# Quarter units in an expert stage: remainders of up to 32 tokens as four column tiles, and another order of the units

## The chip, the core and the metric

One Trainium2 chip, one of its cores. A core has TensorE (PE; its weight loads are listed apart as PEld), VectorE (DVE), ScalarE (ACT), GpSimd (POOL) and SyncE (SP), which run their own instruction streams and wait for each other by semaphores; sixteen DMA engines move data. The metric is the device time of one execution in microseconds; of the kernel before, three runs took 794.92, 795.33 and 796.32 us (median 795.33).

## The reference, cut to what matters

Attention with pooled queries, a gated feed-forward layer (FFN), and then a mixture of experts over 1152 tokens, the part that the change touches:

```python
def _moe2_ref(x, w_gate, w_noise, noise, w1, w2):     # x 1152 x 512, 8 experts, F = 1024
    noisy_logits = x @ w_gate + np.log1p(np.exp(x @ w_noise)) * noise
    top2 = np.argpartition(-noisy_logits, 2, axis=1)[:, :2]
    ...                                               # softmax over the two: top2_w
    for e in range(E):
        for k in range(2):
            mask = top2[:, k] == e
            h = np.maximum(x[mask] @ w1[e], 0.0)      # 512 -> 1024
            out[mask] += top2_w[mask, k, None] * (h @ w2[e])
```

With the reference's inputs (seed 0) the eight experts get 317, 56, 55, 668, 166, 97, 924 and 21 tokens (counted by running the reference). Which tokens go where is only known on the chip at run time.

## The kernel before, in words

The program is one static instruction list per engine. Attention runs to about 270 us, the FFN to about 530 us, and the expert stage from there to the end. Routing (logits, top two, ranks, tables) is worked out in small steps between the matmuls of the FFN and of the first expert unit.

**Blocks and units.** The tokens of each expert are ranked and cut into blocks of 128. A *unit* is one or two blocks of one expert, with that expert's weights (two matrices of 2 MB, loaded in eight pieces of 512 KB). There are fourteen units, numbered 0 to 13, whose kinds are fixed in the list `SEQ`:

- **P**, a pair of blocks (the second with more than 64 tokens): 256 columns at a time.
- **Q**, a full block and a remainder of up to 64 tokens, the *half*.
- **S**, a single block of more than 64 tokens; **H**, a half alone.

Which expert and which tokens a unit gets is data: `r_blocks` gives every pair of blocks a kind by comparing the expert's count with thresholds (`thrs`), ranks the pairs of each kind (`pos`, by a matmul with a triangle), and selects expert numbers (`eb`, `ti`) and token numbers (`gidx`, `sidx`; for halves `gidxh`, `sidxh`, from `r_index`). `NSTAT` says how many units of each kind the static list has. If some kind has more, `more` is 1 and a branch at the end runs further units. Units 0 and 1 are pairs chosen early, from the first 512 tokens.

**P, Q and S blocks** multiply in three passes of split numbers (high and low part, `fp32r`): each weight piece is rounded by ACT (`w_hi`, L106) and subtracted by DVE (`w_lo`, L1037); eight pieces a unit. This split runs five pieces ahead of PE (`LEAD`). Pieces 0 to 3 are up-projections (L1112 for pairs, L1127 for single blocks), pieces 4 to 7 down-projections (L1139).

**Halves** use the weights as loaded (`RAW`, plain fp32; each such matmul is two instructions in the trace). `up_half` (L1147) puts two groups of 64 tokens' results in two column tiles: partitions 0 to 63 take one weight piece, 64 to 127 another. `hh_trans` transposes the result (PE L1158, then a copy, L1162 or L1164). `down_half` (L1171) puts output columns 0 to 255 of the 64 tokens in one column tile and 256 to 511 in the other.

**Order and queues.** `units()` is written out in program order. Two sets of weight buffers, for even and odd units, are reloaded on SP's queue for unit u+2 as unit u frees them: after the split of a piece (P, S), or after `up_half` and `down_half` (Q, H; `reload`). `finish(u)` scales the result (DVE L1201) and adds it into the output in DRAM by an indirect DMA (a scatter, POOL L1202); it stands in the program within unit u+1. All scatters write the same tensor, so each waits until the one before has landed. `gather_x` (POOL L1058) fetches tokens three units ahead, and `x_trans` transposes them (PE L1002, or L1083 for halves).

```python
SEQ = [("P", None)] * 2 + [("P", 0), ("P", 1), ("H", 0), ("P", 2), ("H", 1), ("P", 3), ("Q", 0), ("H", 2), ("Q", 1),
                           ("H", 3), ("Q", 2), ("S", 0)]
```

Of the kernel before, what the change touches and what calls it, by code (L numbers as in the profile page):

```python
# [21 lines left out]
def fused_kernel(ctx, tc, q, k, v, w_gate, w_val, w_out, rms_g,  # L22
                 r_gate, r_noise, noise, e_w1, e_w2, out, dbg=None):
    nc = tc.nc
    P = 128
# [865 lines left out]
    def r_blocks():  # L891
        v, u = rtile("v01", [P, 4]), rtile("u6", [P, 6], BF16)
        ncol = PB["n"][0:NCOL]
        v0, va, vb, mn = (v[0:NCOL, i:i + 1] for i in range(4))
# [14 lines left out]
        pos = rtile("pos", [P, 6])[0:NCOL]  # L909
        pe.matmul(pq[0:NCOL, 0:6], R["lt"][0:NCOL, 0:NCOL], u[0:NCOL], start=True, stop=True)  # L910
        dve.tensor_copy(pos, pq[0:NCOL, 0:6])
# [2 lines left out]
        dve.tensor_tensor(sel, R["i128"][0:NCOL, None, 0:NA].to_broadcast([NCOL, 6, NA]),
                          pos[:, :, None].to_broadcast([NCOL, 6, NA]), op=ALU.is_equal)
        dve.tensor_tensor(sel, sel, kinds[:, :, None].to_broadcast([NCOL, 6, NA]), op=ALU.mult)
# [647 lines left out]
```

## Time and profile before

| | |
|---|---|
| median of three runs | 795.33 us |
| the profiled execution | 794.49 us |
| its span in the trace | 792.6 us |
| PE busy | 758.6 us, 96% of the span |
| DVE, ACT, POOL busy | 525.9, 377.8, 255.2 us |
| PE's granted clock, mean | 0.987 of full speed |
| weight loads of the experts | 112 of 512 KB |

The span runs from the first to the last instruction; 1.9 us of the execution lie around it. Times in the rows are from the span's start. A busy PE is one that has a matmul in flight; how fast it goes is read from the distance between starts. In a timeline, adjacent instructions of one line are merged: the second number is the length of the whole run and xN the number of instructions. "[0.70 <-ACT hs L1130]" says that the engine sat idle for 0.70 us and what ended it.

### The profile page before, as it was taken

The numbers are of one execution on the slowest core, as the hardware profiler recorded it, in microseconds if no ns is written. First come the engines' busy times: TensorE is split into PE (matmuls) and PEld (weight loads), VectorE is DVE, ScalarE is ACT, GpSimd is POOL, SyncE is SP. The second block draws the span as 40 slices with busy tenths as digits, with TensorE's granted clock in tenths as the row PEclk, the third lists the DMA queues.
The fourth block names the chain that finished last, engine by engine and source line by source line (L and its number), as shares of the span: only waits on it lengthen the run. The fifth ranks groups of instructions, "written<-read, shape, count | busy, mean of one in ns | idle before, by whom it ended". The sixth has DMA issues, their size and how long they took to land. (4 is left out here: it accounts for less than half of the span.)

```text
span 792.6 us, 13276 instructions
## 1 busy us (share of the span) xinstructions
PE 758.6 (96%) x5008; PEld 626.4 (79%) x5008; DVE 525.9 (66%) x791; ACT 377.8 (48%) x770; POOL 255.2 (32%) x221
## 2 busy tenths in 40 slices
PE   5999999999999989999999999999999999999993
PEld 4877777777776679988888789997999787877782
DVE  6678778777779867656577745579766564563562
ACT  3665655656667644443242325265535252453460
POOL 8456266375723421222012400102312322313222
PEclk9899999999999999999999999999999999999997
DMA  7344231322131311333023100773997999569922
GB/s 220 88 134 154 63 105 41 95 76 60 46 122 54 107 54 54 107 106 106 14 97 111 51 31 24 258 250 116 350 333 236 265 315 340 169 209 344 330 51 30
DMA packets 72728, 113.28 MB, mean 143 GB/s; under 512 B 7281, under 2 KB 37551, under 8 KB 72656
## 3 DMA queue, kind: packets, MB, share of 16 engines
q1 hardware_dynamic: 67504, 101.55, 39.6%
q0 software_dynamic: 5152, 10.80, 6.1%
q8 instruction: 41, 0.67, 0.4%
q14 instruction: 31, 0.25, 0.1%
HBM read 98.16 MB, written 9.85 MB: 136 GB/s over the span
## 5 line engine op out<-in xcount | busy, mean ns | idle before, releaser
L536 PE MATMUL gv<-XN,ws 128*128 128x256 f32 (+2 forms) x912 | 165.1, 331 | 0.9 <-POOL ws L402 0.9
L536 PEld LDWEIGHTS gv<-XN,ws 128*128 128x128 f32 x912 | 143.7, 189 | 15.0 <-issue 1.8
L193 DVE TENSOR_REDUCE Ql<-s 128x1 fp32r<-128x1152 f32 x72 | 97.3, 1354 | 55.8 <-PE s L188 33.7
L1037 DVE TENSOR_TENSOR wz<-raw,wz 128x1024 fp32r<-128x1024 f32 x80 | 95.9, 1222 | 46.7 <-ACT wz L106 46.5
L204 ACT ACTIVATE et<-st 128x288 f32<-128x288 f32 x288 | 103.5, 417 | 41.4 <-PE st L203 38.9
L202 PE MATMUL st<-QH,KT 128*128 128x288 f32 x288 | 92.3, 335 | 2.4 <-ACT et L204 1.0
L402 POOL TENSOR_TENSOR ws<-wm,ws 128x1024 fp32r<-128x1024 f32 x18 | 43.9, 2437 | 154.5 <-ACT ws L401 139.6
L1139 PE MATMUL py<-wz,hTT 128*128 128x512 f32 x384 | 93.5, 395 | 0.0
L557 PE MATMUL po<-ws,hT 128*128 128x512 f32 x324 | 83.2, 395 | 2.2 <-DVE X L562 2.1
L203 PE MATMUL st<-QlT,KT 128*128 128x288 f32 x288 | 81.8, 298 | 0.0
L106 ACT CAST wz<-raw 128x1024 fp32r<-128x1024 f32 x80 | 81.3, 1046 | 0.8 <-PE py L1139 0.5
L1139 PEld LDWEIGHTS py<-wz,hTT 128*128 128x128 f32 x384 | 70.2, 188 | 13.9
L229 PE MATMUL av<-et,v 128*64 128x288 f32 x576 | 77.4, 412 | 0.5 <-ACT xT L234 0.5
L202 PEld LDWEIGHTS st<-QH,KT 128*128 128x128 f32 x288 | 54.7, 190 | 22.0 <-issue 12.3
L557 PEld LDWEIGHTS po<-ws,hT 128*128 128x128 f32 x324 | 58.9, 188 | 14.2 <-DVE X L562 3.2
L217 DVE TENSOR_TENSOR es<-es,et 128x576 f32<-128x576 f32 x64 | 62.5, 976 | 1.5
L229 PEld LDWEIGHTS av<-et,v 128*64 128x64 f32 x576 | 38.4, 136 | 27.8 <-issue 3.9
L1202 POOL DMA_INDIRECT out_dram<-yo,sidx x16 | 27.3, 1709 | 98.5 <-DVE yo L1201 52.8
L1112 PEld LDWEIGHTS ph<-xgT,wz 128*128 128x128 f32 x480 | 57.9, 188 | 1.0 <-issue 0.8
L1112 PE MATMUL ph<-xgT,wz 128*128 128x256 f32 x480 | 58.4, 282 | 0.0
L203 PEld LDWEIGHTS st<-QlT,KT 128*128 128x128 f32 x288 | 55.2, 192 | 0.1
L546 ACT CAST hT<-sl 128x256 fp32r<-128x256 f32 (+2 forms) x38 | 18.9, 497 | 74.6 <-DVE sl L545 74.6
(282 smaller groups left out, 1135.3 us busy)
## 6 DMA issues: line engine op xcount, KB each, us to landing
raw<-in_moe_w_dram SPq DMA_DIRECT2D x112, 512.0 KB, 8.6
wraw<-in_moe_w_gate_dram SPq DMA_DIRECT2D x6, 1024.0 KB, 5.2
wraw<-in_moe_w_val_dram SPq DMA_DIRECT2D x6, 1024.0 KB, 5.1
wraw<-in_moe_w_out_dram SPq DMA_DIRECT2D x6, 1024.0 KB, 5.0
kraw<-in_k_dram SPq DMA_DIRECT2D x16, 288.0 KB, 4.0
v<-in_v_dram SPq DMA_DIRECT2D x8, 576.0 KB, 4.1
KT<-KT SPq DMA_DIRECT2D x16, 288.0 KB, 3.2
Qraw<-in_q_dram SPq DMA_DIRECT2D x16, 256.0 KB, 4.0
```

The source lines that it names most:

```text
L106: act.copy(o, i)
L193: dve.tensor_reduce(Ql[p % 3][h][:, c, D:D + 1], t[:, :, 0:384], axis=AX.XY, op=ALU.max, negate=True)
L202: pe.matmul(t[:, 0:NG], KT[p, h][:, cs], QhT[p, h][:, n0:n0 + NG], start=True, stop=False)
L203: pe.matmul(t[:, 0:NG], KT2[h][p % NKT[h]][:, cs], QlT[p, h][:, n0:n0 + NG], start=False, stop=True)
L204: act.activation(et[:, h, :], t[:, 0:NG], AF.Exp, scale=SCALE)
L217: eng.tensor_tensor(acc, acc, e, op=ALU.add)
L229: pe.matmul(av[h * D:(h + 1) * D, 0:NG], V[p][:, h, c, :], ET[p, g, c][:, h, :], start=(c == 0), stop=(c == KC - 1))
L536: pe.matmul(t[:, 0:n], w[a][:, d, j * P:(j + 1) * P], XN[hf][b_][:, d, cs], start=(k_ == 0), stop=(k_ == 11))
L557: pe.matmul(pt, HT[f, hf][a][:, j, c0:c0 + P], w[b_][:, j, :], start=(k_ == 0), stop=(k_ == 5))
L1037: eng.tensor_tensor(lo, RAW[u % 2][i], hi.bitcast(F32), op=ALU.subtract)
L1112: pe.matmul(o, w[a][:, d, j * P:j * P + P], XT[u][c][:, d], start=z + d == 0, stop=z == 2 and d == 3)
L1139: pe.matmul(PL[u, "y", k], x[c][:, f0 + d, k * P:k * P + P], w[a][:, d], start=i == 4 and z + d == 0, stop=i == 7 and z == 2 and d == 1)
```

## The change

**Kinds.** A remainder of up to 32 tokens becomes a *quarter*. There are now six kinds of units: P (second block of more than 64), Q (full block and a half, 33 to 64), R (full block and a quarter), S, H (a half alone) and T (a quarter alone). The thresholds grow from three to five, the kinds from six columns to nine, and the columns ranked statically shrink from 12 to 5 for each kind (`NA`). `NSTAT` is 4 P, 1 Q, 2 R, 1 S, 3 H, 1 T; before it was 4 P, 3 Q, 1 S, 4 H. With the counts above, the experts need exactly these: P for experts 0, 3, 6 and 6; R for 3 and 6 (128 + 28 each); Q for 4 (128 + 38); S for 5; H for 0, 1 and 2; T for 7.

**Quarters.** `up_some`, `h_some` and `down_some` replace `up_half`, `hh_trans` and `down_half`. With four parts, the up-projection puts four weight pieces on four column tiles of 32 and is done after one group; one pair of transposes follows; the down-projection writes 128 output columns in each of four tiles. The scatter then writes rows of 128 numbers.

**Order.** P P P P P R P H R S Q T H H instead of P P P P H P H P Q H Q H Q S.

**Overflow.** The further units of the branch are ranked inside the branch (`r_over`); there are 20 (12 P, 8 S) instead of 24.

Core of the diff:

```diff
-    HB = P // 2
-    NA = 12
-    KP, KQ, KS, KH, KP2, KQ2 = range(6)
-    NCU = 6 * NA
-    NSTAT = (4, 3, 1, 4)
+    NK, NA, NO = 9, 5, 12
+    K_P, K_Q, K_R, K_S, K_H, K_T, K_P2, K_Q2, K_R2 = range(NK)
+    O_P, O_S, O_P2 = range(NK, NK + 3)
+    NCU = NK * NA
+    NSTAT = (4, 1, 2, 1, 3, 1, 4, 1, 2)
...
-        thrs = rtile("thrs", [P, 3])
-        for z, o in enumerate((P + HB, P, HB)):
+        thrs = rtile("thrs", [P, 5])
+        for z, o in enumerate((192, 160, 128, 64, 32)):
             dve.tensor_scalar(thrs[:, z:z + 1], thr, float(o), None, op0=ALU.add)
-        dve.tensor_scalar(rtile("hoff", [P, 1]), R["ip"], float(HB), 2.0 * BIG, op0=ALU.is_ge, op1=ALU.add)
...
+        thrs = rtile("thrs", [P, 5])
+        for z, o in enumerate((192, 160, 128, 64, 32)):
             dve.tensor_scalar(thrs[:, z:z + 1], thr, float(o), None, op0=ALU.add)
-        dve.tensor_scalar(rtile("hoff", [P, 1]), R["ip"], float(HB), 2.0 * BIG, op0=ALU.is_ge, op1=ALU.add)
+        off = rtile("off", [P, 2])
+        dve.tensor_scalar(off[:, 0:1], R["ip"], 64.0, 2.0 * BIG, op0=ALU.is_ge, op1=ALU.add)
+        dve.tensor_scalar(off[:, 1:2], R["ip"], 32.0, 4.0 * BIG, op0=ALU.is_ge, op1=ALU.add)
+        for o in (64.0, 96.0):
+            dve.scalar_tensor_tensor(off[:, 1:2], R["ip"], o, off[:, 1:2], op0=ALU.is_ge, op1=ALU.add)
...
-        dve.tensor_scalar(kinds[:, 0:4], wd[:, 5:9], va, None, op0=ALU.mult)
-        yield
-        dve.tensor_scalar(kinds[:, 4:6], wd[:, 3:9:5], vb, None, op0=ALU.mult)
+        dve.tensor_scalar(kinds[:, 0:6], wd[:, 7:13], va, None, op0=ALU.mult)
+        yield
+        dve.tensor_scalar(kinds[:, 6:7], wd[:, 4:5], vb, None, op0=ALU.mult)
+        dve.tensor_scalar(kinds[:, 7:9], wd[:, 11:13], vb, None, op0=ALU.mult)
         dve.tensor_copy(u[0:NCOL], kinds)
...
+        over = [eb[:, NA * z + NSTAT[z]:NA * z + NSTAT[z] + 1] for z in range(6)]
+        for z in range(3):
+            dve.tensor_tensor(v[:, z:z + 1], over[z], over[3 + z], op=ALU.min)
+        dve.tensor_reduce(v[:, 3:4], v[:, 0:3], axis=AX.X, op=ALU.min)
         dve.tensor_scalar(more, v[:, 3:4], NE - 0.5, None, op0=ALU.is_lt)
...
-        tab, tabd = pl.tile([P, P], F32, name="tabs"), pl.tile([P, 2, HB], F32, name="tabd")
+        tab = R["tabs"] = pl.tile([P, P], F32, name="tabs")
+        tabd = [pl.tile([P, P], F32, name=f"tabd{n}") for n in (2, 4)]
         dve.tensor_tensor(tab[0:NCOL], PB["t"][0:NCOL, 0:P], R["tab0"][0:NCOL], op=ALU.add)
-        act.copy(tabd[0:NCOL], tab[0:NCOL, None, 0:HB].to_broadcast([NCOL, 2, HB]))
+        for t, n in zip(tabd, (2, 4)):
+            act.copy(t[0:NCOL].rearrange("p (g c) -> p g c", g=n), tab[0:NCOL, None, 0:P // n].to_broadcast([NCOL, n, P // n]))
...
-        sidh, gidh = rtile("sidxh", [P, 2 * NA], I32), rtile("gidxh", [P, 2 * NA], I32)
-        for z, kind in enumerate((KH, KQ2)):
-            pe.matmul(pd[:, NA * z:NA * z + NA], tabd[0:NCOL].rearrange("p g c -> p (g c)"), sel[:, kind], start=True, stop=True)
-        dve.tensor_scalar(gidh, pd[:, 0:2 * NA], float(BIG), float(BIG - 1), op0=ALU.add, op1=ALU.min)
-        dve.tensor_scalar(sidh, pd[:, 0:2 * NA], 2.0, R["hoff"], op0=ALU.mult, op1=ALU.add)
+        sidh, gidh = rtile("sidxh", [P, 4 * NA], I32), rtile("gidxh", [P, 4 * NA], I32)
+        for z, (n, k) in enumerate(HCOL):
+            pe.matmul(pd[:, NA * z:NA * z + NA], tabd[n // 4][0:NCOL], sel[:, k], start=True, stop=True)
+        dve.tensor_scalar(gidh, pd[:, 0:4 * NA], float(BIG), float(BIG - 1), op0=ALU.add, op1=ALU.min)
+        for z in range(2):
+            o = slice(2 * NA * z, 2 * NA * z + 2 * NA)
+            dve.tensor_scalar(sidh[:, o], pd[:, o], 2.0 + 2.0 * z, R["off"][:, z:z + 1], op0=ALU.mult, op1=ALU.add)
...
+    def r_over(bank):
+        f = X2[:, 6]
+        lim, lo, v3, p3 = f[0:NCOL, 0:NK], f[0:NCOL, 16:16 + NK], f[0:NCOL, 32:35], f[0:NCOL, 36:39]
+        s3 = f[0:NCOL, 64:64 + 3 * NO].rearrange("p (z n) -> p z n", z=3)
+        for z in range(NK):
+            dve.memset(f[:, z:z + 1], float(NSTAT[z]))
...
-    SEQ = [("P", None)] * 2 + [("P", 0), ("P", 1), ("H", 0), ("P", 2), ("H", 1), ("P", 3), ("Q", 0), ("H", 2), ("Q", 1),
-                               ("H", 3), ("Q", 2), ("S", 0)]
-    SEQ = [(a, {"P": ((KP, r), (KP2, r)), "Q": ((KQ, r), (KQ2, r)), "S": ((KS, r),), "H": ((KH, r),)}[a]) for a, r in SEQ]
+    HCOL = ((2, K_H), (2, K_Q2), (4, K_T), (4, K_R2))
+    BLOCKS = {"P": (K_P, K_P2), "Q": (K_Q, K_Q2), "R": (K_R, K_R2), "S": (K_S,), "H": (K_H,), "T": (K_T,)}
+    SEQ = [("P", ((None, 0), (None, 1)))] * 2
+    for a, r in (("P", 0), ("P", 1), ("P", 2), ("R", 0), ("P", 3), ("H", 0), ("R", 1), ("S", 0), ("Q", 0), ("T", 0), ("H", 1), ("H", 2)):
+        SEQ.append((a, tuple((z, r) for z in BLOCKS[a])))
     NU1 = len(SEQ)
-    SEQ += [("P", ((KP, r), (KP2, r))) for r in range(NSTAT[KP], NA)]
-    SEQ += [("P", ((KQ, r), (KQ2, r))) for r in range(NSTAT[KQ], NE)]
-    SEQ += [("S", ((KS, r),)) for r in range(NSTAT[KS], NE)] + [("S", ((KH, r),)) for r in range(NSTAT[KH], NE)]
+    SEQ += [("P", ((O_P, r), (O_P2, r))) for r in range(NO)] + [("S", ((O_S, r),)) for r in range(NE)]
...
-    def half(u, k):
-        return kind(u) == "H" or kind(u) == "Q" and k == 1
...
+    def parts(u, k):
+        z = SEQ[u][1][k][0]
+        return dict((z, n) for n, z in HCOL).get(z, 1)
+
+    def some(u):
+        return kind(u) in "QRHT"
+
+    def split_up(u):
+        return kind(u) not in "HT"
...
-        def up_half(u, a):
-            k = nblk(u) - 1
+        def last_parts(u):
+            return parts(u, nblk(u) - 1)
+
+        def up_some(u, a):
+            m = last_parts(u)
+            n = P // m
             t = pbank("ph")
             for d in range(4):
-                for g in range(2):
-                    pe.matmul(t[HB * g:HB * g + HB, 0:256], XH[u][:, d],
-                              RAW[u % 2][2 * a + g].rearrange("p a (b f) -> p (a b) f", f=256)[:, d],
-                              start=d == 0, stop=d == 3)
+                for g in range(m):
+                    pe.matmul(t[n * g:n * g + n, 0:256], XH[u][:, d],
+                              RAW[u % 2][m * a + g].rearrange("p a (b f) -> p (a b) f", f=256)[:, d],
+                              start=d == 0, stop=d == 3, tile_position=(0, n * g))
...
-        def hh_trans(u, a, eng):
+        def h_some(u, a, eng):
+            m = last_parts(u)
+            n = P // m
             if a == 0:
-                HH[u] = X2[:, 4 + u % 2, 0:8 * HB].rearrange("p (c t) -> p c t", t=HB)
-            pt = pbank("ph") if kind(u) == "H" else bank()
+                HH[u] = X2[:, 4 + u % 2, 0:8 * n].rearrange("p (c t) -> p c t", t=n)
+            pt = bank() if split_up(u) else pbank("ph")
             for j in range(2):
                 pe.transpose(pt[:, j * P:j * P + P], HS[u, "h", a][:, j * P:j * P + P], ident)
-            o = HH[u][:, 4 * a:4 * a + 4].rearrange("p (g j) t -> p j g t", g=2)
-            i = pt[:, 0:2 * P].rearrange("p (j g t) -> p j g t", j=2, g=2)
+            o = HH[u][:, 2 * m * a:2 * m * a + 2 * m].rearrange("p (g j) t -> p j g t", g=m)
+            i = pt[:, 0:2 * P].rearrange("p (j g t) -> p j g t", j=2, g=m)
...
-        def down_half(u):
+        def down_some(u):
             k = nblk(u) - 1
+            m = last_parts(u)
+            n, w = P // m, DM // m
             y = PL[u, "y", k] = pbank("py")
             for c in range(8):
-                for g in range(2):
-                    pe.matmul(y[HB * g:HB * g + HB, 0:256], HH[u][:, c], RAW[u % 2][4 + c // 2][:, c % 2, 256 * g:256 * g + 256],
-                              start=c == 0, stop=c == 7)
+                for g in range(m):
+                    pe.matmul(y[n * g:n * g + n, 0:w], HH[u][:, c], RAW[u % 2][4 + c // 2][:, c % 2, w * g:w * g + w],
+                              start=c == 0, stop=c == 7, tile_position=(0, n * g))
...
-                n, o = (DM // 2, out_h) if half(u, k) else (DM, out)
+                n = DM // parts(u, k)
                 dve.tensor_scalar(yo[:, k, 0:n], PL[u, "y", k][:, 0:n], WV[u][:, 2, k:k + 1], 1.0, op0=ALU.mult, op1=ALU.mult)
-                pool.indirect_dma_start(out=o, out_offset=bass.IndirectOffsetOnAxis(ap=col(u, k, "sidx"), axis=0),
+                pool.indirect_dma_start(out=outs[parts(u, k)], out_offset=bass.IndirectOffsetOnAxis(ap=col(u, k, "sidx"), axis=0),
...
-                if kind(u) == "H":
-                    up_half(u, 0)
-                    up_half(u, 1)
+                if not split_up(u):
+                    na = 4 // last_parts(u)
+                    for a in range(na):
+                        up_some(u, a)
                     reload(u, range(4))
-                    hh_trans(u, 0, dve)
+                    if na == 2:
+                        h_some(u, 0, dve)
                     next_x(u)
-                    hh_trans(u, 1, dve)
+                    h_some(u, na - 1, dve)
...
+                r_over(pbank)
                 units(NU1, len(SEQ))
```

On PE, a Q unit of before (unit 12; raw_52xx are weight pieces, X the transposed half, hs its activations):

```order
L1147 MATMUL ph<-raw_5273,X_3285 64x256 x8
L1147 MATMUL ph<-raw_5274,X_3285 64x256 x8
L1127 MATMUL ph<-wz,xgT 128x256 x12
L1158 MATMUL xt<-ident,hs 128x128 x2
L1127 MATMUL ph<-wz,xgT 128x256 x12
L1158 MATMUL xt<-ident,hs 128x128 x2
L1127 MATMUL ph<-wz,xgT 128x256 x12
L1002 MATMUL xt<-ident,hs 128x128 x4
L1171 MATMUL py<-raw_5275,X_3285 64x256 x4
L1171 MATMUL py<-raw_5276,X_3285 64x256 x4
```

and an R unit of the changed kernel (unit 8):

```order
L1199 MATMUL ph<-raw_5278,X_3285 32x256 x2
L1199 MATMUL ph<-raw_5279,X_3285 32x256 x2
...
L1175 MATMUL ph<-wz,xgT 128x256 x12
L1212 MATMUL xt<-ident,hs 128x128 x2
L1175 MATMUL ph<-wz,xgT 128x256 x24
L1050 MATMUL xt<-ident,hs 128x128 x4
L1227 MATMUL py<-raw_5280,X_3285 32x128 x8
L1227 MATMUL py<-raw_5281,X_3285 32x128 x8
```

The up-projection of the remainder has half as many matmuls, one pair of transposes is gone, and the down-projection has twice as many of half the columns.

On PE, the end of before, from the last down-projection of unit 12's half to the end of unit 13, an S:

```order
L1171 MATMUL py<-raw_5278,X_3285 64x256 x4
L1127 MATMUL ph<-wz,xgT 128x256 x12
L1139 MATMUL py<-wz,hTT 128x512 x6
L1002 MATMUL xt<-ident,hs 128x128 x4
L1139 MATMUL py<-wz,hTT 128x512 x6
L1002 MATMUL xt<-ident,X_3285 128x128 x4
L1139 MATMUL py<-wz,hTT 128x512 x12
L1127 MATMUL ph<-wz,xgT 128x256 x36
L1002 MATMUL xt<-ident,hs 128x128 x4
L1127 MATMUL ph<-wz,xgT 128x256 x12
L1002 MATMUL xt<-ident,hs 128x128 x4
L1139 MATMUL py<-wz,hTT 128x512 x24
```

and of the changed kernel, from the end of unit 10's Q through T (its last rows), H and the last H:

```order
L1187 MATMUL py<-wz,hTT 128x512 x12
...
L1131 MATMUL xt<-ident,xg_5443 128x64 x4
L1212 MATMUL ph<-ident,hs 128x128 x2
L1227 MATMUL py<-raw_5565,X_3285 32x128 x8
...
L1199 MATMUL ph<-raw_5278,X_3285 64x256 x8
L1212 MATMUL ph<-ident,hs 128x128 x2
L1131 MATMUL xt<-ident,X_3285 128x64 x4
L1212 MATMUL ph<-ident,hs 128x128 x2
L1227 MATMUL py<-raw_5280,X_3285 64x256 x4
...
L1212 MATMUL ph<-ident,hs 128x128 x4
L1227 MATMUL py<-raw_5565,X_3285 64x256 x4
```

Three short units now stand at the end, and between the transposes of T and its down-projection no other matmul stands.

On POOL, the last transfers of before (gathers into X, scatters into out_dram):

```order
L1058 DMA X_3285<-XD,gidx 128x516
L1202 DMA out_dram<-yo,sidx 1152x512
L1202 DMA out_dram<-yo,sidxh 2304x256 x2
L1202 DMA out_dram<-yo,sidx 1152x512
L1202 DMA out_dram<-yo,sidxh 2304x256
L1202 DMA out_dram<-yo,sidx 1152x512
```

and of the changed kernel:

```order
L1105 DMA X_3285<-XD,gidxh 128x516
L1259 DMA out_dram<-yo,sidx 1152x512
L1259 DMA out_dram<-yo,sidxh 2304x256
L1259 DMA out_dram<-yo,sidxh 4608x128
L1259 DMA out_dram<-yo,sidxh 2304x256 x2
```

The last scatter was a full block's; now five scatters, of units 10 to 13, follow each other, and the last is a half's.

## Rows read from the trace of the kernel before

**Rows 1.** Busy time by stretch (us); per engine busy (count), then clock, DMA share, GB/s.
```profile
550.00:576.00 26.00, 26.00 (x167) 23.65 (x167) 20.25 (x30) 14.65 (x18) 9.97 (x7) 1.00 1.05 346
700.00:750.00 50.00, 50.00 (x386) 36.22 (x382) 25.41 (x41) 21.70 (x34) 14.16 (x10) 1.00 0.93 296
...
767.00:780.20 13.20, 12.48 (x82) 10.90 (x80) 9.03 (x10) 6.05 (x9) 3.36 (x3) 1.00 0.21 27
780.20:792.60 12.40, 0.00 (x0) 0.00 (x0) 0.75 (x1) 0.00 (x0) 1.55 (x1) 0.58 0.17 23
```

**Rows 2.** Timeline of PE, units 9 to 11: start, length, engine, line, operation, count.
```profile
708.68 3.67 PE L1147 MATMUL ph<-raw,X 128*64 128x256 f32 x32
...
717.35 3.62 PE L1147 MATMUL ph<-raw,X 128*64 128x256 f32 x32
...
722.42 0.38 PE L1158 MATMUL xt<-ident,hs 128*128 128x128 f32 x2
722.56 1.66 PE L1127 MATMUL ph<-wz,xgT 128*128 128x256 f32 x12
...
726.23 3.67 PE L1171 MATMUL py<-raw,X 128*64 128x256 f32 x32
...
738.00 3.67 PE L1147 MATMUL ph<-raw,X 128*64 128x256 f32 x32
```

**Rows 3.** Timeline of PE, one visit each of the two lines with four 32-column tiles.
```profile
64.76 0.74 PE L245 MATMUL sm<-es,ones 128*32 128x320 f32 x8
...
466.49 0.43 PE L679 MATMUL lg<-xrt,wgn 128*32 128x128 f32 x8
```

**Rows 4.** Costliest groups by form, PE: count, busy us, mean ns, idle before.
```profile
L1147 PE MATMUL ph<-raw,X 128*64 128x256 f32 x224 | 25.6, 381 | 0.0
...
L245 PE MATMUL sm<-es,ones 128*32 128x320 f32 x64 | 6.0, 445 | 0.0
...
L679 PE MATMUL lg<-xrt,wgn 128*32 128x128 f32 x32 | 1.7, 285 | 0.0
```

**Rows 5.** Timeline of all engines, end of unit 0 (routing work between its matmuls).
```profile
544.09 0.20 PE L910 MATMUL pq<-u,lt 72*72 72x6 bf16 x1 [0.17 <-DVE u L906]
...
549.56 0.30 ACT L937 COPY tabd<-tabs 72x128 f32<-72x128 f32 x1 [3.45 <-DVE tabs L936]
...
549.91 0.61 PE L947 MATMUL pd<-sel,tabd 72*128 72x12 f32 x4
```

**Rows 6.** Timeline of PE, end of unit 13, the last.
```profile
774.02 0.66 PE L1002 MATMUL xt<-ident,hs 128*128 128x128 f32 x4 [0.70 <-ACT hs L1130]
774.44 5.74 PE L1139 MATMUL py<-wz,hTT 128*128 128x512 f32 x24
```

**Rows 7.** Timeline of POOL: scatters into the output, idle before and releaser.
```profile
641.33 1.57 POOL L1202 DMA_INDIRECT out_dram<-yo,sidx  x1 [6.89 <-DVE wz L1037]
649.57 1.55 POOL L1202 DMA_INDIRECT out_dram<-yo,sidxh  x1 [6.67 <-DMA out_dram<-yo,sidx]
...
772.38 1.55 POOL L1202 DMA_INDIRECT out_dram<-yo,sidx  x1 [5.11 <-DVE yo L1201]
777.83 1.55 POOL L1202 DMA_INDIRECT out_dram<-yo,sidxh  x1 [3.90 <-DMA out_dram<-yo,sidx]
781.75 1.55 POOL L1202 DMA_INDIRECT out_dram<-yo,sidx  x1 [2.37 <-DMA out_dram<-yo,sidxh]
```

**Rows 8.** Chain of work that ended last: start, us, what.
```profile
772.38 4.69 DMA out_dram<-yo,sidx
...
777.83 3.16 DMA out_dram<-yo,sidxh
```

**Rows 9.** Late weight loads: issues from 738 to 757 us; busy time of one stretch.
```profile
raw<-in_moe_w_dram SPq DMA_DIRECT2D x8, 512.0 KB, 9.1
...
747.00:756.00 9.00, 9.00 (x80) 7.40 (x78) 2.02 (x2) 4.23 (x8) 1.57 (x1) 1.00 1.01 336
```

**Rows 10.** Costliest groups of instructions, 550 to 792 us.
```profile
L1037 DVE TENSOR_TENSOR wz<-raw,wz 128x1024 fp32r<-128x1024 f32 x71 | 85.1, 1222 | 46.0 <-ACT wz L106 45.9
...
L1164 DVE COPY X<-ph 128x256 f32<-128x256 f32 x8 | 3.4, 420 | 12.0 <-PE ph L1158 12.0
```

More of the change, by code (lines that the diff above doesn't have):

```diff
@@ L908, in r_blocks @@
         pq = bank_((ps, "gv1", 2), "pq")
[L909 to L911 removed]
+        pos = rtile("pos", [P, NK])[0:NCOL]
+        pe.matmul(pq[0:NCOL, 0:NK], R["lt"][0:NCOL, 0:NCOL], u[0:NCOL], start=True, stop=True)
+        dve.tensor_copy(pos, pq[0:NCOL, 0:NK])
         yield
         sel = R["sel"][0:NCOL]
[L914 to L916 removed]
+        dve.tensor_tensor(sel, R["i128"][0:NCOL, None, 0:NA].to_broadcast([NCOL, NK, NA]),
+                          pos[:, :, None].to_broadcast([NCOL, NK, NA]), op=ALU.is_equal)
+        dve.tensor_tensor(sel, sel, kinds[:, :, None].to_broadcast([NCOL, NK, NA]), op=ALU.mult)
         yield
@@ new lines, in r_index @@
+        for z, (n, k) in enumerate(HCOL):
[10 more added lines that the diff above has]
+            dve.memset(f[:, z:z + 1], float(NSTAT[z]))
+        dve.tensor_tensor(lo, R["pos"][0:NCOL], lim, op=ALU.is_ge)
+        dve.tensor_tensor(lo, lo, R["kinds"][0:NCOL], op=ALU.mult)
+        dve.tensor_reduce(v3, lo.rearrange("p (z n) -> p z n", z=3), axis=AX.X, op=ALU.add)
+        dve.tensor_copy(R["u9"][0:NCOL, 0:3], v3)
+        pq = bank("ph")
+        pe.matmul(pq[0:NCOL, 0:3], R["lt"][0:NCOL, 0:NCOL], R["u9"][0:NCOL, 0:3], start=True, stop=True)
+        dve.tensor_copy(p3, pq[0:NCOL, 0:3])
+        dve.tensor_tensor(s3, R["i128"][0:NCOL, None, 0:NO].to_broadcast([NCOL, 3, NO]),
+                          p3[:, :, None].to_broadcast([NCOL, 3, NO]), op=ALU.is_equal)
+        dve.tensor_tensor(s3, s3, v3[:, :, None].to_broadcast([NCOL, 3, NO]), op=ALU.mult)
+        pv = bank("ph")
+        s3 = s3.rearrange("p z n -> p (z n)")
+        pe.matmul(pv[:, 0:3 * NO], R["em"][0:NCOL], s3, start=True, stop=True)
+        g = X2[:, 7]
+        for i, nm in enumerate(("eb", "ti", "sidx", "gidx")):
+            R[nm + "o"] = g[:, 64 * i:64 * i + 3 * NO]
+            if i:
+                R[nm + "o"] = R[nm + "o"].bitcast(I32)
+        dve.tensor_scalar(R["ebo"], pv[:, 0:3 * NO], float(NE), None, op0=ALU.add)
+        dve.tensor_scalar(R["tio"], R["ebo"], float(NE - 1), None, op0=ALU.min)
+        pi = bank("ph")
+        pe.matmul(pi[:, 0:3 * NO], R["tabs"][0:NCOL], s3, start=True, stop=True)
+        dve.tensor_scalar(R["gidxo"], pi[:, 0:3 * NO], float(BIG), float(BIG - 1), op0=ALU.add, op1=ALU.min)
+        dve.tensor_scalar(R["sidxo"], pi[:, 0:3 * NO], float(BIG), None, op0=ALU.add)
@@ L1021, in experts @@
         xgs = [E0["xg"], X2[:, 0:2]]
-        out_h = out.rearrange("n (g d) -> (n g) d", g=2)
+        outs = {n: out.rearrange("n (g d) -> (n g) d", g=n) for n in (2, 4)}
+        outs[1] = out
         pm = []
@@ L1044, in col @@
             if u < 2:
-                c = 2 * u + k
-                nm += "0"
-            elif half(u, k):
+                t, c = R[nm + "0"], 2 * u + k
+            elif parts(u, k) > 1:
                 z, r = SEQ[u][1][k]
-                c = r + NA * (z == KQ2)
-                nm += "h"
-            else:
-                c = ucol(u, k)
-            return R[nm][:, c:c + 1]
+                t, c = R[nm + "h"], r + NA * HCOL.index((parts(u, k), z))
+            else:
+                t, c = ucol(u, k, nm)
+            return t[:, c:c + 1]
         def gather_x(u):
@@ L1176, in piece @@
                 for k in range(nblk(u)):
-                    if not half(u, k):
+                    if parts(u, k) == 1:
                         down(u, i, k)
@@ L1212, in units @@
         def units(u0, u1, skip=0):
-            todo = [(u, i) for u in range(u0, u1) if kind(u) != "H" for i in range(8)]
+            todo = [(u, i) for u in range(u0, u1) if split_up(u) for i in range(8)]
             def split(n):
@@ L1218, in split @@
                     wsplit(v, j)
-                    if v + 2 < u1 and kind(v) != "Q":
+                    if v + 2 < u1 and not some(v):
                         wload(v + 2, j)
@@ L1262, in units @@
                         continue
-                    if kind(u) == "Q":
+                    if some(u):
+                        na = 4 // last_parts(u)
                         if i == 0:
-                            up_half(u, 0)
-                            up_half(u, 1)
+                            for a in range(na):
+                                up_some(u, a)
                             reload(u, range(4))
-                        if i in (1, 2):
-                            hh_trans(u, i - 1, act)
+                        if 0 < i <= na:
+                            h_some(u, i - 1, act)
                         if i == 3:
-                            down_half(u)
+                            down_some(u)
                             reload(u, range(4, 8))
```

43 lines of the change are left out of this document (21 added, 22 removed).

## The prediction

> **What bounds the kernel now.** I read the busy time by stretch first. In the expert stage PE is busy without a gap (26.00 of 26.00 us, 50.00 of 50.00) at the full granted clock, while the DMA engines are near their limit in places (share 0.93 from 700 to 750 us, 296 GB/s) and DVE has a share to spare [rows 1]. So PE sets the pace, and the weight loads come next. PE stops at 780.2 us, and 12.4 us follow without a matmul [rows 1]. The timeline of PE then gives the price of each unit by the distance of starts: unit 9, an H, lasts from 708.68 to 717.35, 8.67 us, and unit 10, a Q, to 738.00, 20.65 us [rows 2]. Last I read POOL: each scatter is released by the landing of the one before [rows 7].
>
> **Do the units fit?** The counts that stand in the text on the change need exactly 4 P, 1 Q, 2 R, 1 S, 3 H and 1 T besides the two early pairs, as many as the new list has. So fourteen units run, as before, and the same 14 sets of weights are loaded. Two halves of Q units become quarters (R), and one H becomes a T.
>
> **A quarter's up-projection.** A half takes 32 instructions in 3.67 us [rows 2], each 381 ns long [rows 4]. They start in waves of two, one for each column tile; 16 waves give a distance of (3.67 - 0.38) / 15 = 0.219 us for 256 columns. Where the kernel has four tiles of 32 columns, eight instructions of 320 columns take 0.74 us with 0.445 us for one [rows 3, 4]: two waves of four, 0.295 us apart, where the half's pace would be 0.274 (0.219 x 320/256). Eight instructions one after the other would take several times as long as this, so four run abreast at nearly the half's pace. A quarter has eight waves: 0.38 + 7 x 0.219 to 0.236 = 1.91 to 2.03 us. I take 1.95, since the excess of 0.02 looks like the start of a visit: a saving of 1.72 us (1.64 to 1.76).
>
> The Trainium skill's page "TensorE: Matmul & The Clock Gate", section "Measured speedup vs the span model", has three column tiles running 2.38 times as fast as one, not three times. If four tiles kept that loss, an estimate from the page is 3.2 times, and each quarter would save some 0.3 us less, 1 us in the sum. The two waves here lie 0.295 us apart against 0.274 for no loss, so the trace bears out less than half of the page's loss.
>
> **Its down-projection.** 64 instructions of 128 columns, 16 waves of four. The nearest row has eight such instructions in 0.43 us with 0.285 us for one [rows 3, 4], so waves 0.145 us apart, the start of a visit included; at the half's pace per column it is 0.110. That gives 0.285 + 15 x 0.110 to 0.145 = 1.94 to 2.46 us. I take 2.10, between the pace per column and the row without its start. Against the half's 3.67 [rows 2] it saves 1.57 us (1.21 to 1.73).
>
> **R and T.** One pair of transposes fewer is 0.14 us in an R (722.42 to 722.56 [rows 2]). An R is thus 3.43 us shorter than a Q, two 6.9. A T replaces an H and saves the same products, 3.29, and a pair of transposes, 0.3, but it loses cover. In an H the second pair of transposes runs while DVE copies the first; in a T the down-projection must wait for the copy (0.42 us, [rows 10]) and its handoffs: 0.6. Before that the transposes wait for the activation, of which the next unit's transposes hide a part; the last unit of before shows 0.70 us for such a wait uncovered [rows 6], and I take 0.3. Net 2.7 us. **Sum of the quarters: -9.6 us** (from the bounds above, -8.2 to -10.7).
>
> **Order.** The S is no longer last, so its uncovered 0.70 us [rows 6] goes. In its place the last H has no next unit whose transposes cover its waits: +0.7 by the same row. Together 0, -0.7 to +0.7.
>
> **Routing.** Kinds, positions and tables stand between unit 0's matmuls. PE already waits 0.17 us for DVE there [rows 5], and one more small DVE operation stands in that chain and another before the tables: 0.3. The matmuls that make the partial indices double; four instructions took 0.61 us with their latency [rows 5], so +0.3. The second table copy on ACT (0.30 us for the first, [rows 5]) lies beside the matmuls. Taken +0.6; 0 (the selections are narrower, 45 columns for 72) to 1.2. The five added constants on DVE stand in the FFN, where PE paces and DVE waits; nothing, or 0.3 if a step there is just in time.
>
> PE then ends at 780.2 - 9.6 + 0.6 = 771.2 us.
>
> **What is late next: the scatters.** Backwards from 771.2: the last H without a successor's transposes takes some 8.4 us (from 762.8), the H before it 8.2 (754.6), the T 5.5 (749.1). The Q's results are scaled within the T, after its copy, about 753.4, and the first of five scatters can go at 753.7. From a full block's scatter to the next one it took 5.45 us at the quiet end of before and 8.24 us under weight loads [rows 7]; from a half's, 3.92 [rows 7]. So the Q's half starts at 759.2 to 761.9, the T's at 763.1 to 765.8, the first H's (its data ready at 768.5) at 768.5 to 769.7, and the last H's, ready at 772.0, at 772.4 to 773.6. A quarter's scatter, whose rows are half as long, does not stand in the trace: I give it a half's 3.92; up to 5.45 would put the end 1.5 us later. I take 773.0. The last scatter is now a half's, which lands 3.16 us after its start and not 4.69 [rows 8]. In before, the last scatter starts at 781.75 [rows 7], would land at 786.44 with 4.69, and the span ends 6.16 us later. Now: 773.0 + 3.16 + 6.16 = 782.3 us. After PE's end there are 11.1 us instead of 12.4, although the chain of scatters costs 1 us there.
>
> **Weights.** The cover for the short units at the end is the load ahead. The last H's first half is asked for after the T's up-projection (751) and its second after the T's end (754.6). A piece landed 9.1 us after its issue (median) at 336 GB/s [rows 9], 12.5 us for 4.2 MB; so all is there at about 765, and the last H's down-projection begins at about 767.7. The cover is under 3 us; if it is gone, PE waits.
>
> **Time.** The span goes from 792.6 to 782.3, the profiled execution from 794.49 to 784.2; the median of the runs lies 0.84 us above that execution, so 785.0 us.
>
> **Rivals.**
> *Smaller gain* (chance 0.24). R, S and Q now follow each other with no H between, and DVE has to split 8 pieces in an S of about 13.2 us: 8 x 1.222 = 9.8 [rows 10], and with its other work (3 subtractions of 0.69, the scaling and the weights of tokens) over 13 us. For it: that is the whole unit. Against it: the five pieces of lead, and PE was never kept waiting by a split in the Q units before. If each piece of the S were 0.3 us late, +2.4. A down-projection at 2.46 us adds 1.1, a slow quarter's scatter 1.5. Together up to 790; alone 786 to 787.5.
>
> *Larger gain* (0.08). All products at the half's pace per column, no cost in routing, scatters that never queue: 1.1 + 0.6 + 1.0 less, 782.
>
> *Four tiles run no more than two abreast in a long run* (0.05). The lines that have four tiles make only two waves a visit [rows 3], never 16. Then a quarter costs what a half did, and what is left is -0.6 for three pairs of transposes, +0.9 for the T's waits, +0.6 for routing and -1.3 at the end: 794.9, no change. Against it: the two waves are shown, and nothing in them slows.
>
> *The end starves* (slower; 0.04). One mechanism: the last H waits for its second set of weight pieces. Three short units take 22 us of PE, and three sets of weights 37.5 us at 12.5. The forecast lets the T's set and the first H's land before the T starts; if the last sets took 25 us each (168 GB/s, as when all of it queues behind scatters and gathers), the last down-projection would begin at 777.6 instead of 767.7 and the gain is nearly gone; from 26 us on the kernel is slower. Idle PE may cost more: after PE's end the granted clock falls to a mean of 0.58 [rows 1], toward the lower of its two levels, 1.2 GHz. At that level a down-projection of 3.67 us takes twice as long, and the time is 798. The Trainium skill, same page, section "HAM oscillation — how this bites in real kernels", warns of just such waits for DMA between short bursts of matmuls. Against it: 336 GB/s in this very part of before [rows 9], and the order leaves the DMA queue ahead of PE.
>
> *The forecast* (0.59), own range 783 to 788.
>
> **Range and chances.** 781.5 to 790.5 leaves out the two last rivals and the far ends. About 0.2%, 1.6 us, is what the runs can tell from no change. Faster: 0.59 + 0.24 + 0.08, and a little of the third, 0.92; same 0.04; slower 0.04.
>
> **What would show it.** In the changed trace an up-projection of a quarter (L1199, 128x32 weights) takes 1.9 to 2.05 us and its down-projection (L1227) 1.9 to 2.5; an R lasts about 17.2 us and the T 5.5; no instruction of the branch runs; PE ends near 771 and the last scatter starts within 3 us of that. I am wrong if L1199 takes near 3.7 us, if PE waits for raw weights in unit 12 or 13, if splits keep PE waiting in units 8 to 10, or if the last scatter starts more than 4 us after PE's end.

## The result, and the profile after

The changed kernel takes 786.75 us (median of 4 runs, 786.63 to 787.75) where the kernel before took 795.12 in the same session (4 runs, 794.78 to 796.32): a ratio of 0.9895, 95% interval 0.9878 to 0.9912, so 1.05% faster. The forecast was 785.0, the range 781.5 to 790.5. The profiled execution took 786.65 us, its span is 784.6 (before: 794.49 and 792.6).

The timeline of PE after, first the quarters of unit 5 (an R) and a half of unit 7, then the end of the stage (start, length, engine, line, operation, count, idle time before and what ended it):

```profile
646.97 1.93 PE L1199 MATMUL ph<-raw,X 128*32 128x256 f32 x32
...
653.95 1.95 PE L1227 MATMUL py<-raw,X 128*32 128x128 f32 x64
...
664.22 11.13 PE L1160 MATMUL ph<-xgT,wz 128*128 128x256 f32 x96
...
686.80 3.67 PE L1199 MATMUL ph<-raw,X 128*64 128x256 f32 x32
...
746.20 1.93 PE L1199 MATMUL ph<-raw,X 128*32 128x256 f32 x32
...
748.78 0.44 PE L1212 MATMUL ph<-ident,hs 128*128 128x128 f32 x2 [0.25 <-ACT hs L1203]
749.73 1.95 PE L1227 MATMUL py<-raw,X 128*32 128x128 f32 x64 [0.52 <-DVE X L1218]
751.62 3.96 PE L1199 MATMUL ph<-raw,X 128*64 128x256 f32 x32
...
764.33 0.44 PE L1212 MATMUL ph<-ident,hs 128*128 128x128 f32 x2 [0.20 <-ACT hs L1203]
764.70 3.67 PE L1227 MATMUL py<-raw,X 128*64 128x256 f32 x32
```

A quarter takes 1.93 and 1.95 us beside 3.67 for a half [rows 2]. The first R lasts from 646.97 to 664.22, 17.25 us, against a Q's 20.65; the T from 746.20 to 751.62, 5.42 us. PE never waits for raw weights, and it ends at 764.70 + 3.67 = 768.4 us, 11.8 us sooner than before [rows 1].

Yet the span is only 8.0 us shorter. The scatters into the output on POOL, same columns, tell where 3.8 us went; the answering rows of before are [rows 7]:

```profile
743.85 1.55 POOL L1259 DMA_INDIRECT out_dram<-yo,sidx  x1 [7.05 <-DVE wv L1249]
...
750.61 1.58 POOL L1259 DMA_INDIRECT out_dram<-yo,sidx  x1 [3.89 <-DVE yo L1258]
759.93 1.55 POOL L1259 DMA_INDIRECT out_dram<-yo,sidxh  x1 [7.74 <-DMA out_dram<-yo,sidx]
765.75 1.55 POOL L1259 DMA_INDIRECT out_dram<-yo,sidxh  x1 [4.27 <-DVE yo L1258]
770.40 1.55 POOL L1259 DMA_INDIRECT out_dram<-yo,sidxh  x1 [3.10 <-DVE yo L1258]
774.81 1.55 POOL L1259 DMA_INDIRECT out_dram<-yo,sidxh  x1 [2.86 <-DMA out_dram<-yo,sidxh]
```

These are the S's scatter, the Q's full one and its half, then the T's and the two H's. The last starts 6.4 us after PE's end, the span ends 9.8 us after that. The chain of waits (start, length, what), and below it two rows of DVE, show what the last three wait for:

```profile
765.75 3.91 DMA out_dram<-yo,sidxh
...
769.78 0.50 DVE yo L1258
...
770.40 3.65 DMA out_dram<-yo,sidxh
```

```profile
757.11 0.34 DVE L1258 TENSOR_SCALAR yo<-py,wv 128x128 f32<-128x128 f32 x1
...
765.14 0.47 DVE L1258 TENSOR_SCALAR yo<-py,wv 128x256 f32<-128x256 f32 x1
```

The T's results were scaled at 757.11 and the first H's at 765.14, long before their scatters start; the scaling that POOL's rows of 765.75 and 770.40 name is that of the unit behind. Each scatter waits for the landing of the one before and starts some 0.75 us after it (769.66 to 770.40, 774.05 to 774.81). The scaling at 769.78 is the last H's. It waits for the T's scatter, since yo has one buffer for odd and one for even units, but it is done 4.5 us before its scatter can start and costs nothing here.

Two stretches of the trace (per engine busy time and count, then clock, DMA share, GB/s): while the Q's two scatters are under way the DMA engines are nearly full with the last H's weights, issued from 748.14 on; after PE's end there is almost nothing but waiting.

```profile
748.10:764.00 15.90, 15.13 (x180) 10.89 (x176) 2.91 (x9) 2.28 (x7) 3.13 (x2) 1.00 0.93 300
768.40:784.60 16.20, 0.00 (x0) 0.00 (x0) 0.48 (x1) 0.00 (x0) 3.10 (x2) 0.60 0.14 17
```

### The profile page after: what moved, and what is told of

Read it like the earlier page. It is cut to its first block, busy times and chain, and to the rows that moved or that the text cites. A ratio compares the mean times of both kernels' runs of the same rounds, so it can differ in the third digit from the quotient of the medians.

```text
span 784.6 us, 13464 instructions
## 1 busy us (share of the span) xinstructions
PE 746.8 (95%) x5102; PEld 621.4 (79%) x5102; DVE 524.1 (67%) x798; ACT 375.9 (48%) x766; POOL 257.0 (33%) x221
## 5 line engine op out<-in xcount | busy, mean ns | idle before, releaser
L1259 POOL DMA_INDIRECT out_dram<-yo,sidx x16 | 29.7, 1854 | 102.7 <-DVE yo L1258 62.4
L217 DVE TENSOR_TENSOR es<-es,et 128x576 f32<-128x576 f32 x64 | 60.0, 937 | 1.5
```

The source lines that it names most:

```text
L217: eng.tensor_tensor(acc, acc, e, op=ALU.add)
```

## The experiments

Theory A, as it stood after all runs: PE paces the stage up to its end, and the end is a chain of scatters, begun too late and under weight loads. Rival B: the 16.2 us after PE's end are simply what short last units or half scatters cost. Rival C: the gain comes from the order, not from the quarters. The edits are against the changed kernel unless said otherwise.

**Quarters alone, order as near as can be to the old one.**

```diff
-for a, r in (("P", 0), ("P", 1), ("P", 2), ("R", 0), ("P", 3), ("H", 0), ("R", 1), ("S", 0), ("Q", 0), ("T", 0), ("H", 1), ("H", 2)):
+for a, r in (("P", 0), ("P", 1), ("H", 0), ("P", 2), ("H", 1), ("P", 3), ("R", 0), ("H", 2), ("R", 1), ("T", 0), ("Q", 0), ("S", 0)):
```

> Quarters without the new order: P P P P H P H P R H R T Q S, long units between the short ones as in the kernel before. Theory A (the end of the changed kernel is set by its chain of scatters: five in a row, each waiting for the landing of the one before, begun under weight loads, too slow for T, H, H): PE ends at 768.5 to 770.5 us of the span, 0 to 2 later than in the changed kernel, and 11.8 to 12.8 us follow as in the kernel before; 782.5 to 785 us, faster than the changed kernel's 786.7. Rival B (the 16.2 us after PE's last matmul are the price of the last unit itself, of half scatters and of the longer way past the branch, whatever order goes before): 16 us follow again, 786.5 to 788.5. Rival C (the order itself is what gained): slower than 788.

Measured: 791.77 us (790.81 to 792.70), ratio 0.996 (0.9948 to 0.9973). The time that followed PE's end was as A said, 12.8 us, but PE ended at 777.7, and its timeline in R and T shows waits that the expectation did not have:

```profile
731.25 1.22 PE L1187 MATMUL py<-wz,hTT 128*128 128x512 f32 x2 [3.01 <-ACT hTT L1053]
...
741.90 1.96 PE L1227 MATMUL py<-raw,X 128*32 128x128 f32 x64 [1.43 <-DVE X L1218]
```

ACT's row in the same place names the cause: its cast of a weight piece for the next split unit waits for the load, and the cast that PE needs stands behind it.

```profile
729.66 1.04 ACT L106 CAST wz<-raw 128x1024 fp32r<-128x1024 f32 x1 [4.37 <-DMA raw<-in_moe_w_dram]
```

The wait is half of the loss in that R, which takes 23.06 us where the one before it takes 17.00. Behind the wait the granted clock is 0.50, the lower of its two levels, and the last twelve matmuls of the R take 5.94 us, against 2.95 in the changed kernel (743.25 to 746.20):

```profile
731.25:737.19 5.94, 5.79 (x13) 3.64 (x13) 5.91 (x10) 4.28 (x5) 1.46 (x1) 0.50 1.04 363
```

So the quarters alone, in the old order, gave half of the gain or less: shorter units on PE do not shorten the loads, and with a T between two split units PE waits in the first for casts of the second's weights. The miss is mine; this is the starvation that the prediction looked for at the end, in another place. By its time alone the run lies where C was expected (slower than 788); the next one tests C by itself.

**The order alone**, in the kernel before, with halves only:

```diff
-SEQ = [...] + [("P", 0), ("P", 1), ("H", 0), ("P", 2), ("H", 1), ("P", 3), ("Q", 0), ("H", 2), ("Q", 1), ("H", 3), ("Q", 2), ("S", 0)]
+SEQ = [...] + [("P", 0), ("P", 1), ("P", 2), ("Q", 0), ("P", 3), ("H", 0), ("Q", 1), ("S", 0), ("Q", 2), ("H", 1), ("H", 2), ("H", 3)]
```

> The kernel before with its halves, and the short units last: P P P P P Q P H Q S Q H H H. Theory A: PE ends at 779 to 780.5 us of the span (no quarter, nothing shorter); a Q and three H follow each other, five scatters for 26 us of PE, so the chain is 1 to 4 us behind at the end and 12 to 15 us follow; 793 to 797 us, no gain. Rival C (the order gains by itself): under 791.

Measured: 793.56 us (792.64 to 794.45), ratio 0.998 (0.997 to 0.999). PE ends at 778.8 us and 13.6 follow, as A had it. The order by itself is worth 0.2%, so C falls; but 0.2% and 0.4% do not make 1.05%: quarters and order need each other.

**Two scatters left out.** Those of units 11 and 12 are not issued, so their part of the output is missing.

```diff
+                if u in (11, 12):
+                    continue
                 pool.indirect_dma_start(out=outs[parts(u, k)], ...
```

> The changed kernel without the scatters of units 11 and 12 (the T's and the first H's tokens are not added to the output). Theory A: the Q's two scatters have landed by 765 us of the span, the last H's starts at about 769.3, right after PE's end and its scaling, lands 3.7 us later and 6.05 us follow: span 779.1, execution 781.0. Rival B: no change, 786.6.

Measured: 781.74 us, from two runs that lie 2.8 us apart (780.36 and 783.12); the span of the first is 778.4. There the last scatter starts at 768.21, right behind its scaling and 0.8 us after PE's end, instead of 6.4. The end is the chain, as A has it.

**No weight loads for the last unit**, which multiplies with the weights that the T left behind:

```diff
         def wload(u, i):
+            if u == 13:
+                return
```

> The changed kernel with the weight loads of its last unit left out (12 of 1.05 MB pieces, on the queue from about 748 to 764 us); the last unit multiplies with the weights that the unit before it left behind, so the same instructions run on every engine. Theory A, the scatters of the end land late because weight loads stand on the same DMA engines: the scatter of the full unit before (8.6 us in the changed kernel) lands in 4.7 to 5 us and its half (5.1) in 3.2 to 4.0, the last scatter starts at 769 to 771 instead of 774.8, the span ends at 779 to 781, the time is 781 to 783. Rival B, five scatters in a row are that slow by themselves: the landings stay at 8.6 and 5.1 us and the time at 786 to 788. In both TensorE ends at about 768.

Measured: 782.36 us (782.09 to 783.50), span 780.5. What is left out is eight loads of 512 KB; the "12 of 1.05 MB" of the expectation is wrong. POOL's rows, for the same five scatters as above:

```profile
750.88 1.58 POOL L1261 DMA_INDIRECT out_dram<-yo,sidx  x1 [3.81 <-DVE yo L1260]
756.60 1.55 POOL L1261 DMA_INDIRECT out_dram<-yo,sidxh  x1 [4.14 <-DVE X L1220]
760.74 1.55 POOL L1261 DMA_INDIRECT out_dram<-yo,sidxh  x1 [2.60 <-DMA out_dram<-yo,sidxh]
765.91 1.55 POOL L1261 DMA_INDIRECT out_dram<-yo,sidxh  x1 [3.62 <-DVE yo L1260]
770.66 1.55 POOL L1261 DMA_INDIRECT out_dram<-yo,sidxh  x1 [3.20 <-DMA out_dram<-yo,sidxh]
```

From the full scatter to the half it is 5.72 us instead of 9.32, from the half to the T's 4.14 instead of 5.82, and the span is 4.1 us shorter while PE still ends at 764.71 + 3.67 = 768.4. The loads beside them make the scatters late; B falls for this part. The stretch of the loads now reads:

```profile
748.10:764.00 15.90, 15.21 (x184) 10.26 (x176) 2.91 (x9) 2.29 (x7) 4.68 (x3) 1.00 0.26 41
```

**The scaling ahead of the copies in short units**, so that the Q's scatter starts sooner:

```diff
+                    finish(u - 1)
                     if na == 2:
                         h_some(u, 0, dve)
                     next_x(u)
                     h_some(u, na - 1, dve)
-                    finish(u - 1)
```

> The changed kernel with the scaling and scatter of the unit before moved up in H and T units: right after the up-projection is issued, ahead of the copies of the transposed activations on DVE. Theory A: the Q's first scatter starts at 747.5 instead of 750.6 us, partly before the last weight loads, and the whole chain moves up by 3 to 5 us: 781.5 to 783.7. Rival B: the last scatter depends on PE's end alone, 786.6, no change.

Measured: 788.75 us (786.15 to 789.57, 4 runs), ratio 0.9918 (0.9894 to 0.9942): no gain, a miss. In this execution PE was already 1.9 us late when the T began: 0.6 of it stands before unit 1, where the code is the same, and 1.0 in unit 8, which a later run with the same edit does not show; its cause stays open. But the rows of the end show two mechanisms. The Q's scatter could start only 1.2 us sooner by the T's begin, not 3, since the S's was still on its way; and the first H's scaling, now ahead of the last H's copies, held them until its buffer came free, so that PE waited. POOL, then DVE, then PE:

```profile
745.77 1.55 POOL L1259 DMA_INDIRECT out_dram<-yo,sidx  x1 [7.06 <-DVE wv L1249]
751.38 1.58 POOL L1259 DMA_INDIRECT out_dram<-yo,sidx  x1 [2.74 <-DMA out_dram<-yo,sidx]
```

```profile
767.89 0.48 DVE L1258 TENSOR_SCALAR yo<-py,wv 128x256 f32<-128x256 f32 x1 [9.06 <-DMA out_dram<-yo,sidxh]
```

```profile
768.76 3.67 PE L1227 MATMUL py<-raw,X 128*64 128x256 f32 x32 [2.35 <-DVE X L1218]
```

**Short units spread out**, the T last and the loads done before the last two units; then the same with early scaling:

```diff
-... ("R", 0), ("P", 3), ("H", 0), ("R", 1), ("S", 0), ("Q", 0), ("T", 0), ("H", 1), ("H", 2)):
+... ("H", 0), ("P", 3), ("H", 1), ("R", 0), ("R", 1), ("Q", 0), ("S", 0), ("H", 2), ("T", 0)):
```

> Another order of the same units (nothing else changed): four full, a half, a full, a half, the two with quarters, then the two of the other two-part kinds, a half and last the quarter-only unit. The last weight loads are done before the last two units begin, and no short unit stands between two that need late weights. Theory A: TensorE ends at 768 to 769.5 as in the changed kernel, the scatters land in 3.2 to 5 us, 12 to 13.5 us follow TensorE's end, the time is 782 to 784.5. Rival B, the price of the end goes with half and quarter scatters whatever stands beside them: 16 us follow and the time is 786 to 788. Starved as with the first order tried: TensorE ends at 772 or later and the time is above 786.

> The order of the run before it, and the output of the preceding unit is scaled and scattered earlier: ahead of the copies for the down-projection in short units, at the third step instead of the sixth in the unit that begins with a split. Theory A: with no loads beside the scatters each starts as soon as the unit before it is done, 10.4 to 11.5 us follow TensorE's end of 768 to 769.5, the time is 780.5 to 783. Rival: as when this was done in the changed order, the scaling then stands ahead of VectorE's copies and TensorE waits 2 us for them, 783 to 786.

Measured: 788.60 us (788.12 to 789.53) and 787.37 us (786.54 to 789.10). Both miss. In the first, PE ends at 768.07 + 1.95 = 770.0 and 16.9 us follow, by the number nearer to B than to A. But its scatters are late much earlier, where two units with two scatters each follow each other:

```profile
741.40 2.56 POOL L1259 DMA_INDIRECT out_dram<-yo,sidx  x1 [11.35 <-DVE yo L1258]
749.19 1.55 POOL L1259 DMA_INDIRECT out_dram<-yo,sidxh  x1 [5.23 <-DMA out_dram<-yo,sidx]
...
757.68 1.57 POOL L1259 DMA_INDIRECT out_dram<-yo,sidx  x1 [5.62 <-DMA out_dram<-yo,sidxh]
```

The second R's results were complete when the Q began, at 722.78 on PE, but are scaled at the fifth of its eight steps and leave at 741.40; nothing behind them on the chain can catch up. Taking the loads away from the end does not help a chain that is already behind. In the second run the edit leaves that scaling where it was (among the split units it moves the S's alone), and those results leave at 740.15. That led to the last pair.

**The chain begun early, order as changed:** the scaling at the third step of every split unit, and in short units as in the edit above; then the first of these edits alone.

```diff
-                    if u > max(u0, 1) and i == (1 if last else 5 if kind(u) == "S" else 4):
+                    if u > max(u0, 1) and i == (1 if last else 2):
```

> The changed kernel, its order kept, with the output of the preceding unit scaled and scattered at the third step of every split unit (before: the fifth or sixth) and, in short units, ahead of the copies for the down-projection. Theory A, the end is a chain of scatters that was begun too late: the two of the second unit with a quarter start near 721 and 729 us instead of 726.2 and 734.6, that of the quarter-split unit near 738 instead of 743.9, the full one of the last large unit at 747 to 748 instead of 750.6, the last of all at 770.5 to 772 instead of 774.8; TensorE ends at 768 to 769, the span at 780.5 to 782, the time is 782 to 784. Rival, the scatters are spaced by the weight loads' share of the DMA engines alone: starting early only makes each land later, the last starts at 774 to 775 and the time stays at 786 to 788.

> Only the first half of the run before it: third step in the split units, short units as in the changed kernel. Theory A: the full scatter of the last large unit still waits for the scaling at 749.6 us, so it starts at 750.6 and lands near 759, its half near 765, the last scatter starts at 774 to 775: the time stays at 786 to 788. If instead the earlier scatters of the units ahead were what mattered, 782 to 784.

Measured: both edits 782.59 us (782.32 to 783.48, 5 runs), ratio 0.9854 (0.9840 to 0.9867); the first alone 787.57 (786.90 to 788.56). Both as A said. POOL with both edits:

```profile
719.07 2.57 POOL L1259 DMA_INDIRECT out_dram<-yo,sidx  x1 [5.88 <-DVE yo L1258]
728.81 1.56 POOL L1259 DMA_INDIRECT out_dram<-yo,sidxh  x1 [7.17 <-DMA out_dram<-yo,sidx]
736.70 2.31 POOL L1259 DMA_INDIRECT out_dram<-yo,sidx  x1 [4.07 <-DVE yo L1258]
747.16 1.58 POOL L1259 DMA_INDIRECT out_dram<-yo,sidx  x1 [2.35 <-DVE yo L1258]
754.02 1.56 POOL L1259 DMA_INDIRECT out_dram<-yo,sidxh  x1 [5.29 <-DMA out_dram<-yo,sidx]
761.98 1.55 POOL L1259 DMA_INDIRECT out_dram<-yo,sidxh  x1 [6.40 <-DVE yo L1258]
766.01 1.55 POOL L1259 DMA_INDIRECT out_dram<-yo,sidxh  x1 [2.48 <-DMA out_dram<-yo,sidxh]
770.79 1.55 POOL L1259 DMA_INDIRECT out_dram<-yo,sidxh  x1 [3.23 <-DMA out_dram<-yo,sidxh]
```

The S's scatter now starts at 736.70, so the Q's can go at 747.16; the loads still stretch its half (7.2 us in the chain of waits), but the last one starts 4.0 us sooner. The edit in the split units alone brought the S's scatter to 739.24 and left the Q's at 750.79, behind the copies. Each edit removes one of two waits, so neither pays without the other. This version beats both kernels: it is 12.0 us under the one before in the same session, 1.46% faster where the changed kernel is 1.05% faster in its own, so 3 to 4 us are new.

## Why the prediction was right, and where it was not

**The bound and the fit.** Right: PE is busy through the stage, the branch does not run, PE's end moves and the span follows.

**Quarter products.** Right, at the good end of the bounds. By the distance of starts a quarter saves 1.75 and 1.72 us (forecast 1.72 and 1.57). The waves of four, (1.93 - 0.38) / 7 = 0.221 us apart, keep the half's 0.219: four tiles cost nothing against two that the trace can show. On the loss for three column tiles in "TensorE: Matmul & The Clock Gate" of the Trainium skill, section "Measured speedup vs the span model": from two tiles to four no such loss shows here. The rival of two tiles abreast is refuted.

**R and T.** The two R are together 7.3 us shorter than the first two Q of before (6.9 forecast), the T 3.25 shorter than an H of 8.67 (2.7 forecast); its two waits are 0.25 and 0.52 us, with 0.3 and 0.6 forecast. Together 10.5 us, where 9.6 was forecast; the prediction's bounds add up to 8.2 to 10.1, not to its 10.7.

**Order.** Wrong in size: 0, at best -0.7, was forecast; the rows say about -2.0. The three H that remain take 25.5 us instead of 26.95, the five full units after the first 115.7 instead of 116.5, the remaining Q and the S 0.4 more. The order alone, in the kernel before, shows about as much: from unit 1's start to PE's end 224.7 us instead of 227.0. Half of it, 1.0 us, is a wait that I had not seen in the trace of before, in the two H that stood between full units:

```profile
627.87 1.95 PE L1171 MATMUL py<-raw,X 128*64 128x256 f32 x16
630.07 1.95 PE L1171 MATMUL py<-raw,X 128*64 128x256 f32 x16 [0.25 <-DVE X L1164]
631.95 11.79 PE L1112 MATMUL ph<-xgT,wz 128*128 128x256 f32 x96
```

The down-projection of the half was cut in two there: 4.08 us by the distance of starts, and 3.60 after (691.94 to 695.54). DVE's rows give the reason: its second copy (L1164) came behind the operands of both blocks of the next full unit (L1007).

```profile
627.94 1.29 DVE L1007 TENSOR_TENSOR xgT<-xt,xgT 128x512 fp32r<-128x512 f32 x2 [0.63 <-ACT xgT L1005]
...
629.60 0.42 DVE L1164 COPY X<-ph 128x256 f32<-128x256 f32 x1
```

Before an R only one block is full, and the half's copy is in time. **Routing** was sized about right: unit 0, where it stands, takes 31.5 to 31.9 us in the nine executions with the new routing and 31.0 and 31.15 in the two with the old, 0.6 forecast. Of the 0.69 us by which unit 1 starts later (553.87 against 553.18), 0.3 lie before unit 0. PE therefore ended at 768.4, not 771.2.

**The scatters.** This step failed, by the mark the prediction set itself: the last scatter starts 6.4 us after PE's end, not under 4. The step took up to 8.24 us for the full scatter, the row under weight loads, but behind it a half's 3.92 from the quiet end of before, although its own sum of the weights has loads landing until 765. The trace of before had the price, two halves under loads that took 7.85 and 7.98 us from start to next start:

```profile
731.77 1.58 POOL L1202 DMA_INDIRECT out_dram<-yo,sidxh  x1 [7.92 <-DMA out_dram<-yo,sidx]
739.62 2.21 POOL L1202 DMA_INDIRECT out_dram<-yo,sidxh  x1 [6.27 <-DVE wz L1037]
...
747.60 1.57 POOL L1202 DMA_INDIRECT out_dram<-yo,sidx  x1 [4.44 <-DMA out_dram<-yo,sidxh]
```

From the first to the last start it forecast 19.3 us; they took 24.2: 9.32, 5.82, 4.65 and 4.41. Under the loads a half is no quicker to land than a full one is without. The wait of the scaling for a buffer that a scatter two units earlier holds was not in the sum either; it cost nothing here, but 2.35 us of PE in the run with early scaling. The quarter's scatter, which had no row, lands like a half's, in 3.91 us. The run without the last loads shows 3.6 and 1.7 us of it to be contention. The gain on PE was 2.8 us larger than forecast and the end 5.1 us dearer (16.2 against 11.1), so the time came out 1.75 us above the forecast, in its own range: two errors of opposite sign, not a right sum.

**Rivals.** "Smaller gain" has the number, 786 to 787.5, but not by its mechanism: no split kept PE waiting in units 8 to 10. Starvation did not happen in this order; it did, by late weight loads and ACT's order, in the first order tried, and there the lower clock that this rival names cost as much as the wait.

## What to carry to other kernels

When the engine that paces a kernel gets faster, what hangs behind it in a serial chain (here scatters into one tensor, each waiting for the last to land) must be priced under the load that then stands beside it, not at the price of a quiet place. A chain that ends late is mended where it falls behind, units earlier, and with every wait ahead of it at once: two edits that gave nothing or less alone gave 0.4 to 0.5% together. Cutting work on the pacing engine also needs an order that gives the loads their old time.

## What was not expected of the hardware

In the traces of all runs, an accumulating scatter of a half block took 3.2 to 4.4 us to land where the DMA engines moved under 60 GB/s meanwhile and, but for one of 4.3, 6.6 to 8.3 where they moved over 300; a full one 4.6 to 5.4 and 6.2 to 9.4. That they share engines is what "DMA: Bandwidth & Descriptors" of the Trainium skill says, section "Issuing engines are not separate DMA queues"; the run without the last loads agrees, and the size is these traces'.

A full unit's up-projection takes 11.47 us in even units and 11.68 in odd ones (1 to 3 before, 1 to 4 after), and only 11.13 in unit 6 after, where some other runs of the same instructions show 11.5. Why stays open.
